# Reordering products and VectorE work at the end of a fused attention and SwiGLU kernel

## The chip, the cores and the metric

The kernel runs on one NeuronCore of one Trainium2 chip. Such a core has four compute engines that matter here: TensorE (matrix products, into PSUM), VectorE and ScalarE (elementwise work, from PSUM or SBUF), and GpSimd, which here only issues loads. Each has its own stream of instructions, and they wait for one another through semaphores. The metric is the device time of one execution in microseconds (us). In profile lines PE is TensorE, PEld its weight loads, DVE VectorE, ACT ScalarE, POOL GpSimd, SP the engine that issues stores; L670 means line 670 of the kernel before.

## What is computed

Sliding-window attention with a position bias (window 128, 8 batches, 8 heads, 576 positions, 64 per head), and on its output, as 4608 tokens by 512, a gated feed-forward layer of width 1536:

```python
def _attn_ref(q, k, v):                      # cut
    scores = scale * np.matmul(q, k.transpose(0, 1, 3, 2))
    ...
    scores = np.where(mask, scores + bias[None], -1000000000.0)
    attn = softmax(scores)                   # written out in the reference
    return np.matmul(attn, v)

def _moe_ref(x, w_gate, w_val, w_out):
    g = x @ w_gate
    silu = g * (1.0 / (1.0 + np.exp(-g)))
    val = x @ w_val
    return (silu * val @ w_out).astype(np.float32)
```

Inputs and output are float32; the kernel computes its products in float16 with float32 sums.

## The kernel before

The tokens are worked on in nine blocks of 512 (n = 0 to 8). Each block needs the gate and value products (`x @ w_gate`, `x @ w_val`), the elementwise gate, which gives hT, and the output projection `hT @ w_out`. Attention for later tokens runs in between until about two thirds of the run.

Two kinds of product are done by a scheme of Strassen and Winograd: seven products of half-size blocks in place of eight, for some additions of blocks. The output projection uses it from block 1 on. The additions of hT's quarters are made by VectorE in three pieces (c = 0 to 2), four operations each:

```python
    def four_sums(a11, a12, a21, a22, s2, s3, s4):
        return [lambda: nc.vector.tensor_sub(s3, a11, a21),      # L488
                lambda: nc.vector.tensor_add(a21, a21, a22),     # L489: S1, in place
                lambda: nc.vector.tensor_sub(s2, a21, a11),      # L490
                lambda: nc.vector.tensor_sub(s4, a12, s2)]       # L491

    def strassen(n, t):        # one half (t) of block n's rows: a generator of seven parts
        ...                    # cut: A11.. are quarters of hT, B.. of w_out, T1..T4 sums of w_out
        if end:                # the last block: X, Y and p2 in banks of PSUM of their own
            X, Y = (ps_a.tile([P, HC], FP32, name="po", tag="a", bufs=4) for _ in range(2))
            p2 = ps_f.tile([P, HC], FP32, name="p2", tag="gv")
        else:                  # X and Y share one bank
            po = ps_f.tile([P, 2, HC], FP32, name="po", tag="po", bufs=1)
            X, Y = po[:, 0, :], po[:, 1, :]
            ...
        def product(dst, a, b, start=False):
            for m in range(HM):                      # six matmuls of 256 columns, L535
                nc.tensor.matmul(dst, a[:, m, cols], b[:, m, :], ...)
        ...
        product(X, A11, B11, True)                   # first; copied away
        yield
        product(p2, A12, B21, not seeded)            # second
        ...
        yield
        product(X, S2, T2)                           # sixth
        nc.scalar.mul(u2s, X, factor)
        yield
        product(Y, S1, T1, end)                      # fifth
        if end and t:
            nc.vector.tensor_scalar_mul(p5s, Y, factor)
        else:
            nc.scalar.mul(p5s, Y, factor)
        yield
        product(X, S3, T3)                           # seventh
        half_plus(low[:, HC:DM], X, p5s)             # L540, VectorE
        ...                                          # store
        yield
        product(Y, S4, B22)                          # third
        half_plus(top[:, HC:DM], Y, u2s)
        ...
        yield
        product(X, A22, T4)                          # fourth
        ...
```

From block 6 on (`SEVEN_FROM`) the gate and value products use the scheme too, for one unit u of 256 of the 1536 columns at a time (six units a block). X and Y are accumulators of one bank each, four such banks in all:

```python
        def first(u):    # X = G1 A11; Z = copy of X (ScalarE)
        def fifth(u):    # Y = T1 S1;  p5 = copy of Y (ScalarE)
        def second(u):   # Z += G2 A12; s = silu(Z) (ScalarE)
        def sixth(u):    # X += T2 S2; u2 = copy of X (ScalarE)

        def third(u):
            X, Y, Z, p5, u2, s = live[u][:6]
            product(Y, V2, 2 * u * P, S4)
            v_ = supool.tile([P, 2, 256], FP16, name="v1", tag="uu")
            nc.vector.tensor_add(v_, Y, u2)                                          # L663
            nc.vector.tensor_mul(hT[n][:, 2 * u:2 * u + 2, 0:256], s, v_)            # L664

        def seventh(u):
            X, Y, Z, p5, u2, s = live[u]
            product(X, tsum[u][2], 0, S3)
            v_ = supool.tile([P, 2, 256], FP16, name="v2", tag="uu")
            nc.vector.tensor_add(v_, X, p5)                                          # L670
            live[u] += (v_,)

        def fourth(u):
            X, v_ = live[u][0], live[u][-1]
            product(X, tsum[u][3], 0, A22)
            s = supool.tile([P, 2, 256], FP16, name="s2", tag="tt")
            nc.scalar.activation(s, X, AF.Silu)                                      # L678
            nc.vector.tensor_mul(hT[n][:, 2 * u:2 * u + 2, 256:512], s, v_)          # L679
```

The turn of a unit mixes it with the unit before: first (now), seventh (before), fifth, sixth (now), fourth (before), second, third (now); k counts these steps within a block. After every third step one part of the projection of the block before is put in, and sums wait in a list, `later`, from which one or two are taken a step. The last unit closes with second, seventh, third, fourth of its own. Then come the seven parts of the last block's projection for each half t, of which the first part of t = 0 is put in earlier:

```python
        for t in (1, 0, 1, 0, 0, 0, 1, 0, 0, 1, 1, 1, 1):
            next(ends[t])
            yield 0.75
```

From step 60 of the program on, only TensorE's instructions are kept in source order (`tc.manual_schedule`). Those of VectorE and ScalarE are put in order by the compiler's scheduler, which takes the source position as their priority.

Of the kernel before, what the change touches and what calls it, by code (L numbers as in the profile page):

```python
# [23 lines left out]
ET = mybir.EngineType  # L24
# [27 lines left out]
def kernel(  # L52
# [10 lines left out]
    nc = tc.nc  # L63
# [6 lines left out]
    NBLK = NTOK // 512  # L70
# [313 lines left out]
    one = supool.tile([P, 1], FP32, name="one", tag="pin", bufs=1)  # L384
# [82 lines left out]
    T1, T2, T3, T4 = (consts.tile([P, HM, HC], FP16, name=f"T{n}") for n in (1, 2, 3, 4))  # L467
# [25 lines left out]
    def at_once(fs):  # L493
        for f in fs:
            f()
# [11 lines left out]
    def strassen(n, t):  # L507

        h = hT[n]
        A11, A12 = h[:, 0:HM, 0:256], h[:, HM:NMB, 0:256]  # L510
        S1, A22 = h[:, 0:HM, 256:512], h[:, HM:NMB, 256:512]
        S2, S3, S4 = hsum[n]
        cols = slice(t * P, (t + 1) * P)
        end = n == NBLK - 1
        seeded = SEVEN_FROM <= n + 1 < NBLK
        factor = 1.0 if n >= SEVEN_FROM else 0.5
        if end:
# [5 lines that stand above are left out]
            p2 = (ps_f.tile([P, HC], FP32, name="p2", tag="gv") if seeded  # L523
                  else ps_a.tile([P, HC], FP32, name="p2", tag="a"))
        top, low = (opool.tile([P, DM], FP32, name="osb", tag="osb") for _ in range(2))
        if end and t:
            spare = [opool.tile([P, DM], FP32, name="osb", tag="osb") for _ in range(2)]
            p1s, p5s, u2s = spare[0][:, 0:HC], spare[0][:, HC:DM], spare[1][:, 0:HC]
        else:
            p1s, p5s, u2s = (supool.tile([P, HC], FP32, name=i, tag=i, bufs=1)  # L530
                             for i in ("p1s", "p5s", "u2s"))

        def product(dst, a, b, start=False):
            for m in range(HM):
                nc.tensor.matmul(dst, a[:, m, cols], b[:, m, :], start=(start and m == 0),  # L535
                                 stop=(m == HM - 1), skip_group_check=True)

        def half_plus(dst, a, b):
            with tc.high_priority() if n + 1 < SEVEN_FROM else ExitStack():
                nc.vector.scalar_tensor_tensor(out=dst, in0=a, scalar=factor, in1=b,  # L540
                                               op0=ALU.mult, op1=ALU.add)

        product(X, A11, B11, True)
        if seeded:
            nc.scalar.copy(p2, X)
        else:
            nc.scalar.mul(p1s, X, factor)
        yield
        product(p2, A12, B21, not seeded)
        if seeded:  # L550
            nc.vector.tensor_scalar_mul(top[:, 0:HC], p2, factor)
        else:
            half_plus(top[:, 0:HC], p2, p1s)
        if end and t:
            store(n, t, top, 0, HC)
        yield
        product(X, S2, T2)
        nc.scalar.mul(u2s, X, factor)
        yield
        product(Y, S1, T1, end)  # L560
        if end and t:
            nc.vector.tensor_scalar_mul(p5s, Y, factor)
        else:
            nc.scalar.mul(p5s, Y, factor)
        yield
        product(X, S3, T3)
        half_plus(low[:, HC:DM], X, p5s)
        if end and t:
            store(n, t + 2, low, HC, DM, True)
        yield  # L570
        product(Y, S4, B22)
        half_plus(top[:, HC:DM], Y, u2s)
        store(n, t, top, HC if end and t else 0, DM, end)
        yield
        product(X, A22, T4)
        if end:
            nc.vector.tensor_scalar_mul(low[:, 0:HC], X, factor)
        else:
            nc.scalar.mul(low[:, 0:HC], X, factor)
        store(n, t + 2, low, 0, HC if end and t else DM, end)  # L580
        yield
# [31 lines left out]
    later = []  # L613

    def gate_val_by_seven(n):

        x = xT[n]
        A11, A12 = x[:, 0:HK, 0:256], x[:, HK:NKB, 0:256]
        S1, A22 = x[:, 0:HK, 256:512], x[:, HK:NKB, 256:512]
        S2, S3, S4 = xsum.pop(n)  # L620
        hT[n] = hpool.tile([P, NMB, 512], FP16, name="hT", tag="hT")
        live = {}

        def product(dst, w, c0, a, start=False):
            for i in range(2):
                for kb in range(HK):
                    nc.tensor.matmul(dst[:, i, :], w[:, kb, c0 + i * P:c0 + (i + 1) * P], a[:, kb, :],  # L627
                                     start=(start and i == 0 and kb == 0),
                                     stop=(i == 1 and kb == HK - 1), skip_group_check=True)

        def first(u):
            X, Y = (ps_a.tile([P, 2, 256], FP32, name=i, tag="a", bufs=4) for i in ("gX", "gY"))
            Z = ps_f.tile([P, 2, 256], FP32, name="gZ", tag="gv")
            live[u] = X, Y, Z
            product(X, G1, 2 * u * P, A11, True)
            nc.scalar.copy(Z, X)

        def fifth(u):
            Y = live[u][1]
            product(Y, tsum[u][0], 0, S1, True)  # L640
            p5 = epool.tile([P, 2, 256], FP32, name="p5", tag="exc", bufs=5)
            nc.scalar.copy(p5, Y)
            live[u] += (p5,)

        def second(u):
            Z = live[u][2]
            product(Z, G2, 2 * u * P, A12)
            s = supool.tile([P, 2, 256], FP16, name="s1", tag="tt")
            nc.scalar.activation(s, Z, AF.Silu)
            live[u] += (s,)  # L650

        def sixth(u):
            X = live[u][0]
            product(X, tsum[u][1], 0, S2)
            u2 = epool.tile([P, 2, 256], FP32, name="u2", tag="exc", bufs=5)
            nc.scalar.copy(u2, X)
            live[u] += (u2,)

        def third(u):
            X, Y, Z, p5, u2, s = live[u][:6]  # L660
            product(Y, V2, 2 * u * P, S4)
            v_ = supool.tile([P, 2, 256], FP16, name="v1", tag="uu")
            nc.vector.tensor_add(v_, Y, u2)  # L663
            nc.vector.tensor_mul(hT[n][:, 2 * u:2 * u + 2, 0:256], s, v_)  # L664

        def seventh(u):
            X, Y, Z, p5, u2, s = live[u]
            product(X, tsum[u][2], 0, S3)
            v_ = supool.tile([P, 2, 256], FP16, name="v2", tag="uu")
            nc.vector.tensor_add(v_, X, p5)  # L670
            live[u] += (v_,)

        def fourth(u):
            X, v_ = live[u][0], live[u][-1]
            del live[u]
# [5 lines that stand above are left out]
        return {f.__name__: f for f in (first, second, third, fourth, fifth, sixth, seventh)}  # L681

    def seven_steps():
# [21 lines left out]
    def ffn():  # L705

        for n in range(NBLK):
            if n > 1:
                parts = chain(strassen(n - 1, 0), strassen(n - 1, 1))
# [36 lines left out]
            if n > 1:  # L746
                assert next(parts, 0) == 0
        ends = [strassen(NBLK - 1, t) for t in range(2)]
        final = ()
        for n, k, name, which in seven_steps():  # L750
            if k == 0 and n > SEVEN_FROM:
                assert next(parts, 0) == 0
# [9 lines left out]
            if k == 35:  # L762
                later.extend(sums(n, 0))
            if name == "fourth" and which is not None and which[1] > 3:
                if which == (NBLK - 1, 5):
                    at_once(final)
                else:
                    later.extend(sums(which[0], which[1] - 3))
            if n == NBLK - 1 and k == 40:
                final = sums(n, 2)  # L770
                later.append(final.pop(0))
            for _ in range(2 if len(later) > 4 or k >= 39 or k < 7 else 1):
                if later:
                    later.pop(0)()
            if n == NBLK - 1 and k == 41:
                next(ends[0])
                yield 0.75
        assert next(parts, 0) == 0 and not later

        for t in (1, 0, 1, 0, 0, 0, 1, 0, 0, 1, 1, 1, 1):  # L780
            next(ends[t])
            yield 0.75


    loaded = done_t = 0
# [227 lines left out]
```

The softmax here doesn't subtract the row's maximum and nothing guards it: scores larger than these inputs give would overflow.

## Time and profile before

| | |
|---|---|
| time, median of 3 runs | 343.24 us (343.03 to 343.28) |
| span of the profiled execution | 342.1 us |
| granted TensorE clock | 0.999 |
| VectorE busy, 180 to 210 us | 29.16 of 30 us |
| VectorE busy, 210 to 240 us | 29.93 of 30 us |
| VectorE busy, 276 to 288 us | 7.29 of 12 us |
| VectorE busy, 322 to 332 us | 9.61 of 10 us |
| ScalarE busy, 322 to 332 us | 4.95 of 10 us |

In a line of the timeline come the start in us from the span's beginning, the duration, the engine, the line of the kernel, the operation, what it writes and reads, the shape, and how many like it were put together; in brackets stands the engine's idle time before it and who ended it. The table's stretches differ a great deal: VectorE is full in the middle of the run, has room after 250 us, and is full again for ten us just ahead of the end.

### The profile page before, as it was taken

The page shows a single profiled execution, that of the slowest core. Times are in us where ns is not written, and L with a number is a line of the kernel's source. Part 1 is how long each engine was busy: PE and PEld are TensorE (multiplying, and loading weights), DVE is VectorE, ACT ScalarE, POOL GpSimd, SP SyncE. Part 2 cuts the span into 40 slices and gives each one's busy share as a digit, 9 for nine tenths or more (in the row PEclk, how much of TensorE's full clock was granted, in tenths as well). Part 3 has the DMA queues.
Part 4 walks back from the last instruction along what each step waited for, and adds up shares of the span by engine and source line. Part 5 has one row for each costly group of instructions (what it writes and reads, how often), then busy time and mean ns, then how long its engine had stood idle before and what let it go on. Part 6 is the DMA issues. An engine that isn't in the chain of part 4 may idle for free.

```text
span 342.1 us, 7787 instructions
## 1 busy us (share of the span) xinstructions
PE 330.2 (97%) x2983; PEld 218.6 (64%) x2983; DVE 277.3 (81%) x652; ACT 207.0 (61%) x412; POOL 109.6 (32%) x136
## 2 busy tenths in 40 slices
PE   7999999999999999999999999999999999999994
PEld 3484445444455665566655655666788878888884
DVE  5477885999798779998899999999855975775683
ACT  3748676565765675666655557463477667676640
POOL 8978672649755176744017000000000000000000
PEclk9999999999999999999999999999999999999999
DMA  9999999999999999999959932041101101011024
GB/s 151 169 180 177 163 173 150 81 132 160 149 173 143 172 166 161 164 162 147 188 125 100 178 35 79 15 77 35 61 10 53 63 0 64 23 41 63 0 71 116
DMA packets 160037, 37.37 MB, mean 109 GB/s; under 512 B 147328, under 2 KB 155648, under 8 KB 160000
## 3 DMA queue, kind: packets, MB, share of 16 engines
q0 software_dynamic: 118336, 18.62, 84.5%
q1 hardware_dynamic: 40976, 17.64, 28.4%
q10 hardware_dynamic: 688, 0.62, 0.6%
q8 instruction: 23, 0.38, 0.5%
q14 instruction: 14, 0.11, 0.1%
HBM read 37.91 MB, written 9.44 MB: 138 GB/s over the span
## 4 chain that ended last, share of the span: by engine, by line
PE 75%; DVE 14%; ACT 6%; issue 3%; DMA 2%; SPq 0%; DVEq 0%
PE po L535 16%; PE pg L400 14%; PE pv L400 14%; PE gX L627 8%; PE av L348 4%; PE gY L627 4%; PE ps L280 3%; PE po L454 2%; PE p L535 2%; DVE hT L430 2%; PE gZ L627 2%; ACT tt L418 2%; ACT ex L286 2%; DVE uu L419 2%; DMA stage<-in_q_dram 2%
## 5 line engine op out<-in xcount | busy, mean ns | idle before, releaser
L400 PE MATMUL pv<-xT,wv_sb 128*128 128x512 f16 (+2 forms) x320 | 76.5, 358 | 0.6 <-DVE uu L419 0.3
L400 PE MATMUL pg<-xT,wg_sb 128*128 128x512 f16 (+2 forms) x320 | 75.8, 358 | 0.3 <-DVE xT L376 0.2
L418 ACT ACTIVATE tt<-pg 128x512 f16<-128x512 f32 (+2 forms) x70 | 41.3, 590 | 47.7 <-PE pg L400 46.6
L286 ACT ACTIVATE ex<-ps 128x512 f16<-128x512 f32 x96 | 50.0, 606 | 10.5 <-PE ps L280 10.5
L419 DVE SCALAR_TENSOR_TENSOR uu<-tt,pg 128x512 f16<-128x512 f16 (+2 forms) x69 | 45.9, 666 | 10.5 <-ACT tt L418 10.3
L430 DVE TENSOR_TENSOR hT<-uu,pv 128x512 f16<-128x512 f16 (+2 forms) x70 | 46.6, 666 | 3.0 <-PE pv L400 1.3
L185 POOL DMA_DIRECT2D va<-in_v_dram x40 | 34.3, 862 | 36.7 <-PE av L348 30.4
L400 PEld LDWEIGHTS <-wv_sb 128*128 128x128 f16 x320 | 28.3, 98 | 25.1 <-issue 3.2
L535 PEld LDWEIGHTS <-hT 128*128 128x128 f16 x384 | 37.0, 98 | 10.6 <-issue 0.8
L400 PEld LDWEIGHTS <-wg_sb 128*128 128x128 f16 x320 | 28.2, 98 | 23.3 <-issue 2.2
L191 POOL DMA_DIRECT2D kn<-in_k_dram x39 | 33.2, 854 | 21.7 <-DMA kT<-kn 11.2
L191 POOL DMA_DIRECT2D qn<-in_q_dram x39 | 33.3, 860 | 15.3 <-DMA va<-in_v_dram 8.8
L535 PEld LDWEIGHTS <-S 128*128 128x128 f16 x288 | 27.3, 98 | 9.0 <-issue 1.4
L292 DVE TENSOR_TENSOR ex<-ex,m_reg 128x1024 f16<-128x1024 f16 x42 | 28.8, 686 | 3.0 <-ACT ex L286 3.0
L351 DVE TENSOR_TENSOR x<-av,rec 128x256 f16<-128x256 f32 x72 | 28.8, 420 | 0.4
L535 PE MATMUL po<-T,S 128*128 128x256 f16 x192 | 26.5, 273 | 0.6 <-DVE S L490 0.3
L535 PE MATMUL po<-T,hT 128*128 128x256 f16 x192 | 26.0, 273 | 0.1
L679 DVE TENSOR_TENSOR hT<-s,v 128x512 f16<-128x512 f16 x18 | 7.6, 423 | 18.5 <-ACT s L678 18.5
L320 ACT ACTIVATE exc<-psc 128x512 f16<-128x512 f32 x40 | 21.3, 609 | 1.9 <-PE psc L316 1.9
L348 PEld LDWEIGHTS <-ex 128*128 128x128 f16 x384 | 17.4, 97 | 4.6 <-issue 1.2
L348 PE MATMUL av<-va,ex 128*128 128x65 f16 x384 | 19.3, 193 | 0.7 <-ACT ex L286 0.7
L280 PE MATMUL ps<-qT,kT 64*128 64x256 f16 x192 | 16.7, 272 | 0.4 <-DVE qT L223 0.2
(134 smaller groups left out, 537.0 us busy)
## 6 DMA issues: line engine op xcount, KB each, us to landing
out_dram<-osb SPq DMA_DIRECT2D x32, 256.0 KB, 2.6
va<-in_v_dram POOLq DMA_DIRECT2D x32, 128.0 KB, 8.1
qn<-in_q_dram POOLq DMA_DIRECT2D x31, 128.0 KB, 8.6
kn<-in_k_dram POOLq DMA_DIRECT2D x31, 128.0 KB, 8.9
wg_sb<-in_moe_w_gate_dram POOLq DMA_DIRECT2D x6, 256.0 KB, 7.7
wv_sb<-in_moe_w_val_dram POOLq DMA_DIRECT2D x6, 256.0 KB, 8.1
wo_sb<-in_moe_w_out_dram POOLq DMA_DIRECT2D x2, 768.0 KB, 9.7
kn<-in_k_dram POOLq DMA_DIRECT2D x8, 64.0 KB, 7.6
```

The lines of the kernel that those rows point to most:

```text
L185: nc.gpsimd.dma_start(va[rank][p0:p1, :, 0:D], src)
L191: nc.gpsimd.dma_start(t_[p0:p1], src)
L286: nc.scalar.activation(e[:, o:o + 2, :], banks[q4][par], AF.Exp, scale=scale)
L292: nc.vector.tensor_mul(e[:, o, :], e[:, o, :], reg[:, o, :])
L348: nc.tensor.matmul(av[:, j, :], w, val, start=(n == 0), stop=(n == len(todo) - 1))
L351: nc.vector.tensor_mul(x[:, 4 * half:4 * half + 4, :], av[:, :, 0:D], rec.broadcast_to([P, 4, D]))
L400: nc.tensor.matmul(ps[:, c0:c1], w[:, kb, ms], xT[n][:, kb, c0:c1], start=(kb == 0 and c0 == 0), stop=(kb == NKB - 1 and c1 == 512), skip_ ...
L418: nc.scalar.activation(tt, pg[:, c0:c1], AF.Tanh, scale=0.5)
L419: nc.vector.scalar_tensor_tensor(out=uu, in0=tt, scalar=one if (n, m) == PIN else 1.0, in1=pg[:, c0:c1], op0=ALU.add, op1=ALU.mult)
L430: nc.vector.tensor_mul(hT[n][:, m, c0:c1], acted[(n, m)][1][:, c0:c1], pv[:, c0:c1])
L535: nc.tensor.matmul(dst, a[:, m, cols], b[:, m, :], start=(start and m == 0), stop=(m == HM - 1), skip_group_check=True)
L627: nc.tensor.matmul(dst[:, i, :], w[:, kb, c0 + i * P:c0 + (i + 1) * P], a[:, kb, :], start=(start and i == 0 and kb == 0), stop=(i == 1 an ...
```

## The change

Four things are done. In the projection, the fifth product goes ahead of the sixth, and its copy is always ScalarE's. In the gate and value products, the additions after the third and the seventh product are given precedence in the scheduler's order. From step k = 38 of the last block, VectorE's instructions are kept in source order, and the sums of the last two thirds of hT (c = 1, 2) are placed by hand. And the two halves of the last projection take turns in another order. The purpose is that what TensorE needs next be ready sooner, above all where hT's last pieces and their sums feed the last projection.

```diff
+        product(Y, S1, T1, end)
+        nc.scalar.mul(p5s, Y, factor)
+        yield
         product(X, S2, T2)
         nc.scalar.mul(u2s, X, factor)
-        yield
-        product(Y, S1, T1, end)
-        if end and t:
-            nc.vector.tensor_scalar_mul(p5s, Y, factor)
-        else:
-            nc.scalar.mul(p5s, Y, factor)
         yield
 ...
-            nc.vector.tensor_add(v_, Y, u2)
+            with tc.high_priority():
+                nc.vector.tensor_add(v_, Y, u2)
             nc.vector.tensor_mul(hT[n][:, 2 * u:2 * u + 2, 0:256], s, v_)
 ...
-            nc.vector.tensor_add(v_, X, p5)
+            with tc.high_priority():
+                nc.vector.tensor_add(v_, X, p5)
 ...
-        final = ()
+        tail = ExitStack()
 ...
             if name == "fourth" and which is not None and which[1] > 3:
-                if which == (NBLK - 1, 5):
-                    at_once(final)
-                else:
+                if n + 1 < NBLK or k < 39:
                     later.extend(sums(which[0], which[1] - 3))
-            if n == NBLK - 1 and k == 40:
-                final = sums(n, 2)
-                later.append(final.pop(0))
-            for _ in range(2 if len(later) > 4 or k >= 39 or k < 7 else 1):
+            for _ in range(2 if len(later) > 4 or k < 7 else 1):
                 if later:
                     later.pop(0)()
+            if n == NBLK - 1 and k == 38:
+                at_once(later)
+                later.clear()
+                tail.enter_context(tc.manual_schedule(engines={ET.DVE}))
+            if n == NBLK - 1 and k == 39:
+                one, two = sums(n, 1), sums(n, 2)
+                one[0]()
             if n == NBLK - 1 and k == 41:
+                one[1]()
                 next(ends[0])
                 yield 0.75
+            if n == NBLK - 1 and k == 42:
+                two[0]()
         assert next(parts, 0) == 0 and not later
-
-        for t in (1, 0, 1, 0, 0, 0, 1, 0, 0, 1, 1, 1, 1):
+        at_once((two[1], one[2], two[2], one[3], two[3]))
+
+        for t in (1, 0, 1, 0, 1, 0, 1, 0, 0, 1, 0, 1, 1):
             next(ends[t])
             yield 0.75
+        tail.close()
```

## The prediction

> **What bounds the kernel now.** I read the page's shares first, then the waits of TensorE alone, then the timeline around each wait that came up, because the shares only say which engine to ask.
>
> The page, parts 1 and 4 (busy us, share of the span, instructions; then the share of each engine in the chain that ended last):
> ```profile
> PE 330.2 (97%) x2983; PEld 218.6 (64%) x2983; DVE 277.3 (81%) x652; ACT 207.0 (61%) x412; POOL 109.6 (32%) x136
> PE 75%; DVE 14%; ACT 6%; issue 3%; DMA 2%; SPq 0%; DVEq 0%
> ```
> TensorE is busy 97% of 342.1 us. The change removes no product, so it can win only what TensorE loses in waits, and what lies after the last product. Which waits are there? The waits of TensorE, from 60 us on (us in total, times, longest):
> ```profile
> PE gX L627 <- DVE v L670: 0.9, 2, 0.6
> PE po L535 <- DVE S L490: 0.3, 1, 0.3
> PE p L535 <- DVE hT L664: 0.3, 1, 0.3
> ```
> All three have VectorE as their releaser, and all three producers are touched by the diff. These figures are too small by about 0.17 us each: a matmul's record runs on until its pipe is empty. I therefore take start to start. An undisturbed group of six 256-column products occupies 0.66 us in the chain of waits, so 0.109 us a product; a group of four 0.44 us. The first of the two long waits, in the timeline:
> ```profile
> 275.82 0.93 PE L535 MATMUL po<-T,S 128*128 128x256 f16 x6
> 275.89 0.41 DVE L490 TENSOR_TENSOR S<-hT 128x512 f16<-128x512 f16 x1
> 276.22 0.68 DVE L663 TENSOR_TENSOR v<-gY,u 128x512 f16<-128x512 f32 x1
> 276.82 0.41 DVE L491 TENSOR_TENSOR S<-hT,S 128x512 f16<-128x512 f16 x1
> 277.03 0.60 PE L627 MATMUL gX<-m_reg,kT 128*128 128x256 f16 x4
> 277.16 0.42 DVE L664 TENSOR_TENSOR hT<-s,v 128x512 f16<-128x512 f16 x1
> 277.49 0.68 DVE L670 TENSOR_TENSOR v<-gX,p 128x512 f16<-128x512 f32 x1
> 278.23 0.60 PE L627 MATMUL gX<-xT,kT 128*128 128x256 f16 x4 [0.60 <-DVE v L670]
> ```
> The reader is to see that the addition L670 frees gX for the fourth product and starts only at 277.49, although its own product (started 275.38, 0.60 long) was complete at 275.98. VectorE was not idle: it did L490, L663, L491 and L664 first, and of these only L490 had a product waiting for it. The wait costs 278.23 - 277.03 - 0.44 = 0.76 us. The same view at 306.16 (group before started 305.30): 0.42 us. The end of the kernel:
> ```profile
> 328.68 0.68 DVE L663 TENSOR_TENSOR v<-gY,u 128x512 f16<-128x512 f32 x1
> 329.08 0.60 PE L535 MATMUL p<-wo_sb,hT 128*128 128x256 f16 x4
> 329.46 0.43 DVE L664 TENSOR_TENSOR hT<-s,v 128x512 f16<-128x512 f16 x1
> 329.95 1.05 PE L535 MATMUL p<-wo_sb,hT 128*128 128x256 f16 x8 [0.26 <-DVE hT L664]
> 330.83 0.97 PE L535 MATMUL po<-T,S 128*128 128x256 f16 x6
> 331.40 0.11 PEld L535 LDWEIGHTS <-S 128*128 128x128 f16 x2 [0.26 <-DVE S L490]
> ```
> and in the chain of waits (start, us, what):
> ```profile
> 331.00 6.74 PE po L535 x60
> ```
> That is sixty products with nothing between them. In the timeline, four of six products of the first block's second product run, then two wait for hT: 329.95 - 329.08 - 0.44 = 0.43 us. The sixth product then waits for S2: 0.97 instead of 0.82 us, 0.15. After that TensorE runs free until 337.73; a last VectorE copy, the store and the closing fill the rest, 4.3 us.
>
> **What the Trainium skill says.** "TensorE: Matmul & The Clock Gate", section Back-to-back issue gap, gives 262 cycles for 256 columns at 2.4 GHz, that is 0.109 us; the trace agrees (0.66 us for six). So I claim no gain inside groups. "Perfetto Trace Analysis", section Optimization Strategy, asks for the gaps of the engine that should be saturated and for making their dependencies start sooner; this is what the diff does. "PSUM — Partial Sum Buffer", section PSUM bank collisions raise a hardware error, says that any two engines on one bank must be kept apart. X and Y of one output block share a bank except in the last block, so every product there waits for the copy of the one before, whichever of the two products is first; the trace before shows one such wait (108.14 us, for the copy p5s). "VectorE: DVE Perf Modes", section The DRAIN you can't avoid, says that a dependent read on the same engine needs a semaphore; the trace shows the price: L663 to the dependent L664 is 0.78 us start to start (328.68 to 329.46), while an independent successor follows after 0.60 us (276.22 to 276.82).
>
> **The change, part by part.**
>
> (a) Fifth product ahead of the sixth, in the seven earlier blocks that are projected by seven products. The number of products and copies is the same. The fifth reads S1, which is the second of the four sums in source order (L489); the sixth reads S2, the third (L490). So waits for L490 should vanish, as S1 is there one sum earlier. Start to start I find three outside the last block: at 142.13 us 0.48 (group of 141.21, four products 0.44), at 216.60 0.08, and at 276.36 0.11 (0.93 against 0.82 above). At 142 us S1 is ready by 140.81 (L489 starts at 140.39, 0.42 long) and the group starts 141.21. But VectorE is busy 27.5 of 30 us between 120 and 150 us and 29 to 30 of 30 between 180 and 240: time that TensorE wins there it may lose again at the next VectorE result. I count half of 0.56, 0.28, and 0.11 at 276 in full. Sum 0.39.
>
> (b) Precedence for the additions L663 and L670, in the blocks from 247 us on. Nothing is added. In the order above L663 can go at about 275.1 (its product ended 275.11) and L670 as soon as its product is done and the instruction in progress lets it, about 276.0 to 276.3. Its 0.68 us end by 277.0, before 277.47, when TensorE wants gX. So the whole 0.76 and, likewise, the 0.42 at 306.16 go: L670 could follow L663 (304.15) at 304.75, ending 305.43, ahead of 305.74. I count 0.70 + 0.42 = 1.12, keeping 0.06 for a rest. What moves back are sums and the multiplication L664, each 0.42, by two places, about 1.2 us at most; products that read them lie more than that behind.
>
> (c) The end. The copy p5s of the second column block goes from VectorE (0.42) to ScalarE (0.38); ScalarE is mostly idle after 330 us. VectorE is put in source order after the sixth product of the last unit. With the busy times above (0.34 from start to start of f16 operations, 0.60 after an addition) I step through it: multiplication of the fourth product of unit 4 when its silu ends, 326.2; one sum 326.55; addition L670 326.9 (TensorE needs it by 327.99); one sum 327.5; L663 at 328.18, as soon as its product ends (327.56 + 0.60), not at 328.68; L664 328.96, ending 329.39. TensorE wants hT at 329.52: the 0.43 wait goes, with 0.1 to spare. Then a sum 329.3, the last multiplication 329.65, S1 of the last third 330.1 to 330.5. The new turn of products takes both second products (329.08 and 329.73), then the fifth of each column block (330.39; it needs that S1 at 330.83), then the sixth of each at 331.70, by which S2 (ends 331.2) is long there: the 0.15 goes too. The tightest step further on is the seventh product, which follows the two sixths: 331.70 + 0.82, then the ScalarE copy 0.38, is 332.93 against 333.00. The last copy and store are of the same sizes, so they shift with the last product. Sum 0.58.
>
> **Sum.** 0.39 + 1.12 + 0.58 = 2.09 us.
>
> Against it I set 0.4 us: VectorE and ScalarE are ordered by the compiler's scheduler from 60 us on, and a changed source gives another order everywhere. The unplanned waits that the present order has between 150 and 240 us are 0.08 to 0.19 us each, five of them; two or three more of them are 0.4. So 343.24 - 2.09 + 0.4 = 341.5 us.
>
> **Rivals.**
>
> 1. VectorE is the bound between 180 and 240 us, and giving the additions precedence, or moving the sums, only trades one wait for another. For: VectorE at 29 to 30 of 30 us there. Against: precedence is for the part from 247 us on, where VectorE is busy 59.3 of 91 us (252 to 343 us), so there is room. If it holds, only (c) and a part of (b) remain: 342.5.
>
> 2. Source order on VectorE stalls it: an instruction that waits for ScalarE holds the ready ones behind it. For: the multiplications L679 waited 18.5 us in total for their silu from 240 us on, up to 2.0 us at once. Against: in the source the sums stand between, and my steps find only waits of about 0.3 us. If it holds, the tail loses 0.5 to 1 us instead of winning 0.58: 342.6 to 343.1.
>
> 3. The stores set the end. The new turn puts the 256 KB store of the first block's last rows 0.65 us later, close to the two last pairs of 64 KB. Before, stores landed 2.0 to 2.8 us after issue (issues from 325 us on, medians). If they queue, 0.2 to 0.4 us of the gain are lost: 341.8.
>
> 4. All goes as planned with no new wait, and the mid-run gain is kept whole: 343.24 - 2.4 = 340.8.
>
> **Range and chances.** The rivals span 340.8 to 343.1, and none of them reaches 2% (6.9 us): all TensorE waits from 60 us on that anything here could remove are under 3 us together. Range 340.7 to 342.9. Faster by over 2%: 0.01. Within 2%: 0.97. Slower by over 2%: 0.02, for a schedule that goes badly wrong through the run.
>
> **What would show it.** Right: no TensorE wait on v L670's counterpart; none on the last hT or on S2 in the end; VectorE's addition starting within 0.1 us of its product's end there; some ninety products back to back at the end; the last product about 2 us earlier than 337.7. (a) is right if no group of S products is over 0.85 us long around 142 and 276 us. Wrong: a new wait of TensorE for the ScalarE copies in the end, or for S1; an end later than 4.6 us after the last product; or waits of TensorE between 60 and 240 us that grew by over 0.5 us, which would mean that the scheduler's new order and not the diff's purpose sets the time.

## The result, and the profile after

The changed kernel takes 341.63 us (median of 6 runs, 341.34 to 342.01), the kernel before 343.05 us (6 runs) on the same chip: a ratio of 0.9958, 95% interval 0.9945 to 0.9971. It is faster, by 1.0 to 1.9 us, and within 2%. The prediction was 341.5 us, from a kernel before of 343.24 us: a change of 1.7 us, where 1.42 was measured.

The page of the changed kernel, the same two lines of parts 1 and 4:
```profile
PE 329.5 (97%) x2983; PEld 218.8 (64%) x2983; DVE 276.7 (81%) x651; ACT 207.3 (61%) x413; POOL 109.8 (32%) x136
PE 84%; DVE 6%; ACT 5%; issue 1%; DMA 1%; ACTq 0%; DVEq 0%
```
The busy times have hardly moved; what moved is the chain: VectorE's share of it fell from 14% to 6% and TensorE's rose from 75% to 84%. The waits of TensorE from 60 us on:
```profile
PE av L348 <- ACT ex L286: 0.7, 2, 0.5
PE po L535 <- ACT u2s L561: 0.3, 1, 0.3
PE px L374 <- DVE x L351: 0.2, 1, 0.2
```
None of the three waits that were shown of before is left. The first and third belong to attention and were there before; the second is the old wait at 108 us, now for u2s instead of p5s, as the two copies have changed places. A rest of one wait is below this list's threshold and shows in the timeline (lines 661, 662, 669 are 663, 664, 670 of before):
```profile
273.88 0.60 PE L624 MATMUL gY<-m_c,wv_sb 128*128 128x256 f16 x4
274.58 0.42 DVE L489 TENSOR_TENSOR hT<-hT 128x512 f16<-128x512 f16 x1
274.93 0.42 DVE L551 TENSOR_SCALAR osb<-p 128x256 f32<-128x256 f32 x1
275.19 0.82 PE L535 MATMUL po<-T,hT 128*128 128x256 f16 x6
275.26 0.68 DVE L661 TENSOR_TENSOR v<-gY,u 128x512 f16<-128x512 f32 x1
275.86 0.42 DVE L490 TENSOR_TENSOR S<-hT 128x512 f16<-128x512 f16 x1
276.19 0.68 DVE L669 TENSOR_TENSOR v<-gX,p 128x512 f16<-128x512 f32 x1
276.28 0.60 PE L624 MATMUL gX<-m_reg,kT 128*128 128x256 f16 x4
276.93 0.60 PE L624 MATMUL gX<-xT,kT 128*128 128x256 f16 x4
```
The group of projection products is 0.82 us long, not 0.93: it is the fifth now and reads hT. The addition L669 ends 276.87 and the wait for it is 276.93 - 276.28 - 0.44 = 0.21 us, where it was 0.76. L661 itself starts 0.78 us after its product's end (273.88 + 0.60), behind a sum and a copy, in spite of its precedence. The end:
```profile
326.47 0.69 DVE L661 TENSOR_TENSOR v<-gY,u 128x512 f16<-128x512 f32 x1 [0.30 <-PE gY L624]
327.26 0.43 DVE L662 TENSOR_TENSOR hT<-s,v 128x512 f16<-128x512 f16 x1
327.36 1.47 PE L535 MATMUL p<-wo_sb,hT 128*128 128x256 f16 x12
328.67 1.47 PE L535 MATMUL po<-T,hT 128*128 128x256 f16 x12
335.42 0.42 DVE L574 TENSOR_SCALAR osb<-po 128x256 f32<-128x256 f32 x1 [0.16 <-PE po L535]
```
L661 starts when its product ends (in brackets: VectorE idle, released by gY), and from 327.36 on TensorE runs without a hole. The chain of waits says the same in one line:
```profile
327.52 1.31 PE p L535 x12
328.83 6.56 PE po L535 x60
```
The last VectorE copy starts at 335.42 and the span ends at 339.9 us, 4.5 us later; before it was 337.75 and 342.1 us, 4.3 us.

The span fell by 2.2 us but the time by 1.4: the profiled execution of before took 343.85 us, 0.8 above the median. About 0.5 us of the difference lies before 30 us, in code that the change does not touch: there TensorE lost 8.1 us in the profile of before and 7.6 in this one, and among the later runs both figures occur, whatever the kernel.

For the experiments I use one sum throughout, called **lost time**: for all successive products from 60 us on, start to start less 0.417 ns a column, where that is over 15 ns. It is 11.48 us before and 9.50 after; most of what remains belongs to attention's small products and is none of this change's business. Differences of it are what counts.

### The profile page after: what moved, and what is told of

Its sections match the earlier page's. It is cut to its first block, busy times and chain, and to the rows that moved or that the text cites. A ratio compares the mean times of both kernels' runs of the same rounds, so it can differ in the third digit from the quotient of the medians.

```text
span 339.9 us, 7782 instructions
## 1 busy us (share of the span) xinstructions
PE 329.5 (97%) x2983; PEld 218.8 (64%) x2983; DVE 276.7 (81%) x651; ACT 207.3 (61%) x413; POOL 109.8 (32%) x136
## 4 chain that ended last, share of the span: by engine, by line
PE 84%; DVE 6%; ACT 5%; issue 1%; DMA 1%; ACTq 0%; DVEq 0%
PE po L535 18%; PE pg L400 16%; PE pv L400 15%; PE gX L624 9%; PE gY L624 4%; PE av L348 4%; PE ps L280 4%; PE p L535 3%; PE po L454 2%; PE gZ L624 2%; PE px L374 2%; ACT tt L418 2%; ACT ex L286 2%; PE psc L316 1%; DVE hT L430 1%
```

## The experiments

All were timed against the kernel before on the same chip. The results first.

| kernel | lost time, us (change) | median, us | before, us | ratio, 95% interval |
|---|---|---|---|---|
| a_alone | 12.93 (+1.45) | 344.69 | 343.19 | 1.0042 (1.0030 to 1.0054) |
| b_alone | 11.05 (-0.43) | 342.80 | 343.19 | 0.9988 (0.9982 to 0.9995) |
| c_alone | 10.80 (-0.68) | 342.95 | 343.19 | 0.9992 (0.9984 to 1.0001) |
| whole | 9.48 (-2.00) | 341.67 | 343.19 | 0.9951 (0.9940 to 0.9963) |
| ab | 11.91 (+0.43) | 343.67 | 343.34 | 1.0010 (1.0002 to 1.0018) |
| turn_old | 11.51 (+0.03) | 343.53 | 343.34 | 1.0004 (0.9995 to 1.0012) |
| no_manual | 9.96 (-1.52) | 342.13 | 343.34 | 0.9968 (0.9955 to 0.9980) |
| end_sixth_first | 9.98 (-1.50) | 341.88 | 343.34 | 0.9958 (0.9946 to 0.9970) |
| turn_old_copy | 10.92 (-0.56) | 342.70 | 343.05 | 0.9990 (0.9982 to 0.9998) |
| early_p4 | 9.58 (-1.90) | 341.65 | 343.27 | 0.9948 (0.9934 to 0.9962) |
| split_store | 9.48 (-2.00) | 341.43 | 343.27 | 0.9947 (0.9933 to 0.9960) |
| late_sums | 9.48 (-2.00) | 341.62 | 343.27 | 0.9947 (0.9934 to 0.9960) |

### The parts, one at a time

**a_alone**: fifth ahead of sixth, with everything else as before.
```diff
+        product(Y, S1, T1, end)
+        ...                      # copy p5s, on VectorE in the second half of the last block
+        yield
         product(X, S2, T2)
         nc.scalar.mul(u2s, X, factor)
         yield
-        product(Y, S1, T1, end)
-        ...
```


> The kernel before with the fifth product ahead of the sixth everywhere, nothing else. Theory (each part removes TensorE waits of its own, and they add up): the waits for S2 at 142, 216, 276 and 331 us go, the long ones at 278 (0.76), 306 (0.42) and 330 us (0.43) stay; 0.3 to 0.5 us faster. Rival 1 (VectorE is the bound between 180 and 240 us and takes it back): same time within 0.1 us, and the waits of TensorE between 60 and 240 us sum to as much as before. Rival 2 (the gain is an accident of the scheduler's new order): anything from 0.5 us slower to 1.5 us faster, with waits at new places.

Measured: 1.5 us slower. The waits for S2 are gone as expected (lost time between 60 and 240 us 9.06 against 9.37 before), but the end has two waits that were not there. The waits of TensorE from 240 us on:
```profile
PE po L535 <- ACT osb L564: 1.1, 1, 1.1
PE gX L627 <- DVE v L670: 1.0, 2, 0.7
PE po L535 <- ACT u2s L564: 0.5, 1, 0.5
PE p L535 <- DVE hT L664: 0.3, 1, 0.3
```
Line 564 is the copy u2s (in the second half it goes to a spare osb). Sixth and seventh product both add into X, and the copy lies between them. Before, the fifth product, into Y, ran meanwhile; with the fifth moved ahead and the old turn, sixth and seventh of one half stand side by side. Start to start the two waits are 0.64 and 1.28 us. None of the three expectations named this. In the rest of the run nothing was won beyond those 0.3 us: the 0.11 at 276 us went, and the next wait for gX grew from 0.76 to 0.87. The edit reaches the last block too, which part (a) of the prediction does not include; fifth first in the seven earlier blocks alone was not run.

**b_alone**: precedence for the two additions, nothing else (the diff is that of the change).

> The kernel before with precedence for the additions after the third and seventh product, nothing else. Theory: the waits at 278 and 306 us (0.76 and 0.42) go but for 0.2, those at 142, 276, 330 and 331 us stay; 0.9 to 1.1 us faster. Rival 1: the sums that are moved back make TensorE wait for S2 or S4 instead, 0.3 us faster or less. Rival 2: the order changes elsewhere too and the waits below 240 us differ by over 0.3 us from those before.

Measured: 0.4 us faster, interval 0.2 to 0.6. The long waits for the addition are gone, and others stand in their place: 0.69 us at 277 and 0.25 us at 305 us, for S2. In the timeline (L664 and L672 are the two additions here):
```profile
275.86 0.60 PE L535 MATMUL po<-T,S 128*128 128x256 f16 x4
275.92 0.68 DVE L664 TENSOR_TENSOR v<-gY,u 128x512 f16<-128x512 f32 x1
276.52 0.41 DVE L490 TENSOR_TENSOR S<-hT 128x512 f16<-128x512 f16 x1
276.99 0.39 PE L535 MATMUL po<-T,S 128*128 128x256 f16 x2 [0.53 <-DVE S L490]
```
The addition went ahead of L490, and the sixth product, which comes first here, wanted S2. Rival 1 of the expectation holds in kind, if not in its figure (0.3 us or less). What the whole change has and this one lacks is the fifth product first.

**c_alone**: only the end is changed.
```diff
+        for f in (fifth_, sixth_) if end else (sixth_, fifth_):   # change: fifth first everywhere
+            f()
+            yield
...                                                                # and no precedence
```


> The kernel changed with parts a and b undone outside the last block's projection: sixth ahead of fifth again in blocks 1 to 7, no precedence. What is left is the end: VectorE in source order, sums by hand, new turn, fifth ahead of sixth in the last block alone. Theory: waits at 330 (0.43) and 331 us (0.15) go, those at 142, 276, 278 and 306 us stay; 0.5 to 0.6 us faster. Rival (the end wins nothing, since the stores set it): the last product is 0.57 us earlier and the end is not, same time within 0.1 us.

Measured: no wait of TensorE is left at the end (lost time 0.68 us less, as expected), but the time is 0.24 us less, with an interval from 0.03 us slower to 0.55 faster. I come back to the difference under the stores.

**whole**: the changed kernel again, on the chip of its parts.

> The changed kernel as it is, on the same chip as its parts. Theory: 1.4 to 2.0 us faster, the sum of the three parts within 0.3 us. Rival (the parts share one gain, or one of them spoils another): 0.5 us or more away from their sum.

Measured: 1.52 us faster. The three parts add up to 0.87 us slower (+1.50 - 0.39 - 0.24), so the sum is off by 2.4 us: the rival holds, and my theory that each part takes away waits of its own falls.

New theory: the parts lean on one another. Precedence needs the fifth product first, and the fifth first needs the new turn at the end. The next four kernels test it.

### Which part needs which

**ab**: a and b together, the end left as it was.
```diff
+        product(Y, S1, T1, end)      # ahead of product(X, S2, T2), as in a_alone
...
+            with tc.high_priority():  # as in the change
+                nc.vector.tensor_add(v_, Y, u2)
```


> The kernel before with the fifth product ahead of the sixth and with precedence for the additions, the end left as it was. New theory (the parts lean on one another): precedence alone only moved the wait from gX to S2, and with the fifth product first S2 is not needed yet, so at 276 to 306 us no more than 0.2 us of waits is left, as in the whole change; but in the old turn at the end the waits of 0.64 and 1.28 us for the copy u2s stay, and the 0.42 for hT. Waits from 60 us on 11.8 against 11.5 us before: 0.3 us slower than before, within 0.3. Rival (the parts add up): 1.5 slower from a, 0.4 faster from b, 1.1 us slower.

Measured: 0.33 us slower than before, lost time 11.91 us (expected: 0.3 and 11.8). At 277 us 0.21 is left and at 305 us nothing, where b_alone had 0.69 and 0.25. So once the fifth product is first, precedence takes away 1.02 us of lost time (a_alone 12.93, ab 11.91), near the 1.12 that I had counted for it. The waits of 0.43, 0.64 and 1.28 us at the end stayed.

**turn_old**: the changed kernel with the old turn.
```diff
-        for t in (1, 0, 1, 0, 1, 0, 1, 0, 0, 1, 0, 1, 1):
+        for t in (1, 0, 1, 0, 0, 0, 1, 0, 0, 1, 1, 1, 1):
```


> The changed kernel with the turn of the last fourteen parts as it was before; VectorE in source order, sums by hand and fifth first as in the change. New theory: sixth and seventh product, which both use X, stand side by side again, so TensorE waits for the copy u2s, 0.6 us in the first half and, where the copy stands behind ScalarE's issues of stores, about 1.2 in the second: 1.6 to 2.0 us slower than the changed kernel, about as long as the kernel before. Rival (source order and the hand-placed sums are what the end wins by): at most 0.3 us slower than the changed kernel.

Measured: 343.53 us, as long as before (interval 0.9995 to 1.0012), 2.03 us more lost time than the changed kernel. The second wait in its timeline:
```profile
333.56 0.82 PE L535 MATMUL po<-T,S 128*128 128x256 f16 x6
333.63 1.38 ACTq L446 DMA_DIRECT2D out_dram<-osb  x2
335.05 0.39 ACT L561 ACTIVATE osb<-po 128x256 f32<-128x256 f32 x1 [2.22 <-PE po L535]
335.49 0.82 PE L535 MATMUL po<-T,S 128*128 128x256 f16 x6 [1.11 <-ACT osb L561]
```
The sixth product is done at 334.38; ScalarE's computing part is idle for 2.2 us, and still the copy starts only at 335.05. What stands between is the second line: ScalarE's sequencer issues two stores until 335.01. The bracket's releaser, the product, had long been done.

**turn_old_copy** puts this to the test: that copy goes to VectorE, which issues no stores.
```diff
         product(X, S2, T2)
-        nc.scalar.mul(u2s, X, factor)
+        if end and t:
+            nc.vector.tensor_scalar_mul(u2s, X, factor)
+        else:
+            nc.scalar.mul(u2s, X, factor)
```


> The changed kernel with the old turn, and the copy u2s of the second half on VectorE. With the old turn and that copy on ScalarE, TensorE lost 0.64 us for the first half's copy and 1.28 for the second's. Theory (the second copy stood behind ScalarE's two issues of stores, 1.38 us together): on VectorE, which issues no stores, the second wait shrinks to 0.65 us, the length of a bare copy between two products of one accumulator; 0.6 us faster than with the copy on ScalarE, 1.2 us slower than the changed kernel. Rival (both waits are the price of the copy, and the second is longer because more is going on at the end): the wait stays over 1 us.

Measured: 0.68 us in place of 1.28 for this wait, lost time 0.59 us less than with the copy on ScalarE, and 0.35 us faster than before. The same place:
```profile
334.17 0.42 DVE L562 TENSOR_SCALAR osb<-po 128x256 f32<-128x256 f32 x1 [0.23 <-PE po L535]
334.65 0.82 PE L535 MATMUL po<-T,S 128*128 128x256 f16 x6 [0.51 <-DVE osb L562]
```
So 0.6 us of the long wait were the issues, and the rest is the copy between two products of one accumulator with nothing else put between: 0.64 us for the first half's on ScalarE, 0.68 for this one on VectorE. The new turn takes both halves' fifth and sixth products before the first seventh, so each copy has another product beside it, and all four copies are past before ScalarE issues its first store.

**no_manual**: the changed kernel without source order on VectorE.
```diff
-                tail.enter_context(tc.manual_schedule(engines={ET.DVE}))
```


> The changed kernel without the source order on VectorE; sums placed where the change has them, new turn. Theory: the scheduler puts sums ahead of the addition L661 again and hT comes late, so 0.2 to 0.45 us of waiting for hT at 328 us is back and the time is that much longer than the changed kernel's. Rival (where the sums stand in the source is enough): the same within 0.1 us, with no wait of TensorE after 300 us.

Measured: 0.43 us of waiting for hT is back, lost time 0.48 us more than in the changed kernel. Where the sums stand in the source was not enough. VectorE in its timeline:
```profile
325.91 0.60 PE L624 MATMUL gY<-m_reg,wv_sb 128*128 128x256 f16 x4
326.23 0.42 DVE L490 TENSOR_TENSOR S<-hT 128x512 f16<-128x512 f16 x1
326.69 0.42 DVE L491 TENSOR_TENSOR S<-hT,S 128x512 f16<-128x512 f16 x1
327.03 0.68 DVE L661 TENSOR_TENSOR v<-gY,u 128x512 f16<-128x512 f32 x1
327.82 0.43 DVE L662 TENSOR_TENSOR hT<-s,v 128x512 f16<-128x512 f16 x1
```
The scheduler pulled two sums, later in the source, in front of L661, although L661 has precedence; its product ends at 326.51, so 0.5 us were lost. In time the two kernels are not told apart (0.9968 and 0.9951, the intervals overlap); the lost time tells them apart.

**end_sixth_first**: the changed kernel with the last block's projection as before (sixth first, old turn, second p5s on VectorE), source order and hand-placed sums kept.
```diff
+        for f in (sixth_, fifth_) if end else (fifth_, sixth_):
...
+        for t in (1, 0, 1, 0, 0, 0, 1, 0, 0, 1, 1, 1, 1):
```


> The changed kernel with the last block's projection as before: sixth ahead of fifth, the second copy p5s on VectorE, the old turn. Kept are source order and hand-placed sums, and parts a and b in the other blocks. Theory: the wait for hT (0.43) is gone, but S2 is needed 0.65 us after the second product starts and comes at about 331.2 on the clock of the kernel before, so the sixth product waits 0.35 to 0.5 us for it; no wait for u2s, since the fifth product stands between. 0.3 to 0.5 us slower than the changed kernel, 1.0 faster than before. Rival (any use of the old turn costs ScalarE's store issues): over 1 us slower than the changed kernel.

Measured: no wait for hT and none for u2s; 0.44 us of waiting for S2, in two pieces, as the sixth product wants it first:
```profile
328.61 0.38 PE L535 MATMUL po<-T,S 128*128 128x256 f16 x2
329.15 0.73 PE L535 MATMUL po<-T,S 128*128 128x256 f16 x4 [0.16 <-DVE S L490]
```
So at the end, source order with the hand-placed sums is worth the 0.43, and fifth first with the new turn a like amount of lost time. But the time is 1.46 us below before, the whole change's 1.52: half a microsecond of lost time more, and not measurably slower. It also shows that fifth first in the earlier blocks does not need the new turn; only in the last block does it.

### The stores

Some of the lost time that the changed kernel saves is not in its time. The change in time less the change in lost time is +0.48 us in whole, +0.44 in c_alone and +0.31 in no_manual, all with the new turn; with the old turn it is less (a_alone +0.05, b_alone +0.04, ab -0.10, end_sixth_first +0.04, turn_old +0.16, turn_old_copy +0.21). One alone is within its interval or hardly outside it. The place where it could go is the end, behind the last product. From the last VectorE copy's start to the span's end it is 4.5 us in the changed kernel, 4.3 in the kernel before and 4.0 in end_sixth_first (335.83 to 339.8). The 64 KB stores that ScalarE issues, from 328 us on (count, KB each, median us from issue to landing), of the kernel before (first line) and of the changed kernel:
```profile
out_dram<-osb ACTq DMA_DIRECT2D x3, 64.0 KB, 2.6
out_dram<-osb ACTq DMA_DIRECT2D x3, 64.0 KB, 2.9
```
and of end_sixth_first:
```profile
out_dram<-osb ACTq DMA_DIRECT2D x3, 64.0 KB, 2.3
```
Same sizes and counts. With the new turn the 256 KB store of the first half's last rows (two of 128 KB) is issued just ahead of the last two pairs of 64 KB. Two kernels tried to mend it.

**early_p4**: that store one place earlier.
```diff
-        for t in (1, 0, 1, 0, 1, 0, 1, 0, 0, 1, 0, 1, 1):
+        for t in (1, 0, 1, 0, 1, 0, 1, 0, 0, 0, 1, 1, 1):
```


> The changed kernel with the fourth product of the first half one place earlier in the turn, so its 256 KB store is issued 0.65 us earlier and only 64 KB stores follow. In the runs so far the end came 4.6 to 4.8 us after the last product's start with the new turn and 4.3 to 4.6 with the old one. Theory (the stores of the new turn crowd the end, 0.25 us): back to 4.4 us, against one or two new waits of at most 0.1 us each, since seventh and fourth of one half have a single product between them: 0.1 to 0.3 us faster than the changed kernel. Rival (the differences at the end are chance): same or 0.1 us slower.

**split_store**: that store in two column halves, the first as soon as the seventh product is copied.
```diff
-        if end and t:
+        if end:
             store(n, t + 2, low, HC, DM, True)
...
-        store(n, t + 2, low, 0, HC if end and t else DM, end)
+        store(n, t + 2, low, 0, HC if end else DM, end)
```


> The changed kernel with the last rows of the first half stored in two column halves, the first as soon as its seventh product is copied. Same bytes, two more issues. Theory (bytes in flight at the end count): end after last product 0.2 us shorter, 0.2 us faster than the changed kernel. Rival (the issues of ScalarE and SyncE, 0.5 to 0.7 us each, fill their queues, and the count of issues matters): 0 to 0.3 us slower.

Measured: from the last product's start to the end 4.54 and 4.52 us, against 4.84 in whole; early_p4 pays 0.1 us in two waits (0.08 and 0.03), as expected. In time neither is told from the changed kernel: 0.9948 and 0.9947 against 0.9951, each give or take 0.0013. Nor from late_sums below, which was timed beside them with the stores of the changed kernel: 0.9947.

The same stretch does not support the pattern above. It is 4.63 us in the kernel before, 4.77 and 4.84 in the two profiles of the changed kernel, but only 4.58 in c_alone and in no_manual, which have the new turn and miss 0.44 and 0.31 us. So the traces give the stores 0.14 to 0.21 us of the gain, from one execution each, and no time confirms it; where the rest of the missing half microsecond goes is open.

### The rest of the wait at 277 us

**late_sums**: the third and fourth sum of a block's last third enter the list after the seventh product, to let the addition go first.
```diff
-                    later.extend(sums(which[0], which[1] - 3))
+                    four = sums(which[0], which[1] - 3)
+                    later.extend(four[:2] if k == 4 else four)
+            if k == 8 and n > SEVEN_FROM:
+                later.extend(four[2:])
```


> The changed kernel with the third and fourth sum of a block's last third put into the list after the seventh product of the next block's first unit, in place of four steps earlier. Theory: the last wait for gX (0.21 us at 276.9 us) goes, as L490 no longer stands ahead of the addition; S2 is still there in time. 0.2 us faster than the changed kernel and no TensorE wait over 0.1 us after 245 us. Rival: the sixth product then waits for S2, same time.

Measured: a miss; lost time 9.48 us as without it, and the wait is still 0.2 us. VectorE's timeline shows why:
```profile
275.39 0.68 DVE L661 TENSOR_TENSOR v<-gY,u 128x512 f16<-128x512 f32 x1
275.99 0.41 DVE L490 TENSOR_TENSOR S<-hT 128x512 f16<-128x512 f16 x1
276.32 0.68 DVE L669 TENSOR_TENSOR v<-gX,p 128x512 f16<-128x512 f32 x1
```
L490 still goes in front of L669, which has precedence and stands earlier in the source. It looks as if the scheduler, in its own reckoning, took L669 as not ready yet; I only infer that. Source order on VectorE in this part, as at the end, was not tried.

## Why the prediction was right, and where it was right by luck

The time (341.5 predicted, 341.63 measured) and the place of every gain are as predicted. By its steps:

**(a), 0.39 us.** Lost time between 60 and 240 us fell by 0.28, exactly the half of 0.56 that was counted, and the 0.11 at 276 us went. The waits at 142 (0.48) and 217 us (0.08) vanished; new small ones of 0.13 us, at 143 and 217 us, took half of it back. That it is lost again at a later result was foreseen; that it was just half is luck, as the half was a guess. What the step left out is the last block: taken over there with the old turn, fifth first costs 1.92 us of lost time (a_alone).

**(b), 1.12 us.** Measured 0.98: all of the 0.43 at 306 us, and 0.55 of the 0.76 at 278 us. The 0.21 that stayed is where the step failed, and its sign (no wait on L670's counterpart) was not met: the step had let L663 go when its product ended and L670 when its own did. L661 waited 0.78 us behind L489 and L551, and L490 went in front of L669. Its sentence that the products which read the sums "lie more than that behind" holds only because (a) put the fifth product first. Alone, (b) gave 0.4 us, and rival 1 in its second form (one wait traded for another) is what happened to it.

**(c), 0.58 us.** Measured 0.57, wait by wait. The step-by-step times were met within 0.1 us: L663's counterpart started 0.04 us after its product's end, hT was ready before it was wanted, and the tightest step, the seventh product after its copy, left no wait. That step was indeed the tight one: turn_old, which takes the slack away, loses 0.64 and 1.28 us. Rival 2 (source order stalls VectorE) did not occur.

**The 0.4 us set against.** Right in size by luck. It was meant for two or three new waits under a new scheduler order; only two of 0.13 us came, and these are within (a)'s half already. Yet the time fell by 1.42 and 1.52 us, for 1.98 and 2.00 us of lost time. Of this missing half microsecond, rival 3 (the stores) has 0.14 to 0.21 us in the traces. To that extent the sentence of step (c) that the last store would shift with the last product failed: from the last product's start to the end it is 4.77 us, where it was 4.63. The rest stays open. A further 0.19 us of the hit is the kernel before, 343.05 us beside the changed one and not 343.24.

So the sum of removed waits was sound (2.09 predicted, 1.94 in the trace over these places), and the deduction hit its size without its cause. The deeper miss is in the form of the argument: a sum of three independent parts. The runs show that they lean on one another: precedence (b) takes away 0.43 us of lost time alone and 1.02 after (a), and fifth first in the last block, which is in (c), costs 1.92 us there without the new turn.

## What to carry to other kernels

When an engine's order is changed to free one wait, ask at once who was served in that place before: here precedence for an addition only moved TensorE's wait to a sum, until the consumer of that sum was moved as well. Between two products that add into one accumulator and have a copy between them, keep another product, and keep such copies off an engine that is issuing stores at that time. At gains of a few tenths of a percent, the lost time of the bounding engine, taken start to start, separates causes that the times alone don't; it does not replace them, since here half a microsecond of it never reached the time.

## What the runs showed of the hardware that was not expected

Two stores of 128 KB issued from ScalarE took its sequencer 1.38 us in turn_old, and a copy behind them started 0.67 us after its product had ended, with the computing part idle: a wait of TensorE of 1.28 us against 0.68 for the same copy on VectorE. The Trainium skill, "DMA: Bandwidth & Descriptors", section Issuing engines are not separate DMA queues, calls the time to initiate a transfer usually small against the transfer itself. Here the two issues took 0.56 and 0.72 us, against a median of 2.8 us from issue to landing, and they were on the path.

A wait reads shorter in the list of waits than it is: 0.5 and 1.1 us listed for 0.64 and 1.28 us lost, as the record of the products before runs on past the time at which the next can start: six have a record of 0.82 us, and the next follows after 0.66. "Perfetto Trace Analysis", section Summary: the profiler window per engine type, says that a matmul's end is an estimate; these 0.16 us fit that, and do not prove it.
